# A decode kernel on one core: neighbouring matmuls of the key stage share a weight load, and SyncE waits for the store last

## The chip, the cores and the metric

The kernel runs on one core of a Trainium2 chip. Its time is the device time of the program in microseconds (us); the span of a profile is the time from the first to the last instruction that the profiler saw, about 2 us less (132.1 us in an execution of before that took 133.93 us). PE is the tensor engine (PEld its weight loads), DVE the vector engine, ACT the scalar engine, SyncE or SP the engine that issues the transfers here. Numbers of the form L309 are lines of the kernel.

"Fast" and "slow" are states that an execution is put into by its time.

## The reference, cut to what matters

One token is decoded. Branch A is attention over the last 4,096 cached positions with 32 query heads on 16 key heads; branch B is a dense layer with gelu. A sigmoid gate mixes them.

```python
q = (x @ wq)                                   # 576 x 4096
scores = einsum("bhqd,bhkd->bhqk", q, k) * Dh ** -0.5
o = einsum("bhqk,bhkd->bhqd", softmax(scores), v)
a = o.reshape(...) @ wo                        # 4096 x 576
b = gelu(x @ w1 + b1) @ w2 + b2                # 576 x 4608, 4608 x 576
return g * a + (1 - g) * b
```

With one token, every weight and every cached key and value is read once and used once or twice: 53.6 MB have to come from device memory (the page of before counts 53.62 MB read).

## The kernel before

The transfers are issued in one order by SyncE: w1, wq, eight blocks of keys, the first half of w2, the values, wo, the second half of w2. The key stage takes each block of keys as it lands, transposes it on DVE in two halves, and multiplies it on PE:

```python
for g in range(NG):
    k_t = big.tile([P, 2, SL, Dh], BF16, name="k_t", tag="CDBA"[g])
    for f in range(2):
        ...
        nc.sync.dma_start(out=k_t[:, f, :, :]..., in_=src)
        kt = kt_pool.tile([P, SL * Dh], BF16, name="kt", tag="kt")
        for u in range(2):
            nc.vector.transpose(...)           # L300: two halves of a block
        for u in range(4):
            for j in range(4):                 # L309: 16 matmuls of 512 columns
                nc.tensor.matmul(
                    s_ps[:, u * 512 : (u + 1) * 512]...,
                    lhsT=qz[:, h0 // 2, j, :],
                    rhs=kv[:, u * SL // 4 : (u + 1) * SL // 4, j // 2, :, j % 2],
                    ...
                )
```

Each of these matmuls has its own weight load (`lhsT`), although only four different weights occur in a block. The end of the kernel:

```python
# L415, L417: wo in two pieces, the second half of w2 in pieces of 10, 6 and 2 rows
for r in range(RO):
    y_add(ov[:, r : r + 1], wo_t[:, r, :])               # two matmuls of 288 columns each
for f in range(NJ, NF):
    y_add(gt[:, f : f + 1], w2_t[:, f, :], stop=(f == NF - 1))
out_row = const.tile([1, D], BF16, name="out_row")
nc.scalar.copy(out=out_row[:, DH:D], in_=y_out[1])
nc.vector.tensor_copy(out=out_row[:, 0:DH], in_=y_out[0])
nc.sync.dma_start(out=out..., in_=out_row[:])            # the store
```

After the last line the framework adds the end of the program: SyncE waits for eleven semaphores (counters that the trace shows raised by finished work and waited for), the store's, 103, among them, and then all engines meet in a barrier.

## Time and profile before

| | before |
|---|---|
| time, median (lowest to highest, 5 runs) | 134.09 us (134.00 to 134.19) |
| span of the profile | 132.1 us |
| moved, mean rate | 53.78 MB, 407 GB/s |
| weight loads of the key stage | 128, 12.8 us busy |
| last piece of w2 used from | 128.25 us |
| store issued, span ends | 129.94 us, 132.14 us |

The table of stretches gives for each stretch of time its length, the busy time of each engine (with the number of instructions), the clock granted to PE as a share, the share of time that the transfer engines were busy, and their rate in GB/s.

```profile
44.00:73.00 29.00, 22.71 (x98) 9.16 (x99) 25.09 (x12) 0.00 (x0) 0.00 (x0) 1.00 1.02 432
91.00:113.60 22.60, 14.04 (x498) 13.57 (x495) 0.37 (x3) 0.00 (x0) 0.00 (x0) 0.50 1.00 423
```

The transfers are busy throughout these stretches (shares 1.02 and 1.00), at 432 and 423 GB/s, while PE and DVE have gaps (22.71 and 25.09 us busy of 29.00 in the first, 14.04 and 0.37 of 22.60 in the second), and the chain that ended last is 67% transfers. So the kernel is bound by its reads.

The groups of the key stage, by line, engine, operation and shapes, with count, busy time in us and mean ns of one, and behind the second bar the idle time of the engine before them and what ended it:

```profile
L300 DVE STREAM_TRANSPOSE kt<-k_t 128x2048 f32<-128x2048 f32 x16 | 36.0, 2290 | 9.7 <-DMA k_t<-in_A_k_cache_dram 9.7
L309 PE MATMUL s_ps<-kt,qz_flat 128*128 128x512 bf16 x128 | 32.3, 399 | 9.2 <-DVE kt L300 9.2
L309 PEld LDWEIGHTS <-qz_flat 128*128 128x128 bf16 x128 | 12.8, 100 | 28.3 <-issue 14.7
```

DVE waits for keys to land, PE waits for DVE, and nothing waits for a weight load. The timeline around one half of a block (start, length, engine, line, what, count, and in brackets the idle time before) shows the pace:

```profile
61.33 1.89 PE L309 MATMUL s_ps<-kt,qz_flat 128*128 128x512 bf16 x8 [0.30 <-DVE kt L300]
61.33 1.61 PEld L309 LDWEIGHTS <-qz_flat 128*128 128x128 bf16 x8 [0.58 <-issue]
61.68 4.50 DVE L300 STREAM_TRANSPOSE kt<-k_t 128x2048 f32<-128x2048 f32 x2 [0.41 <-DMA k_t<-in_A_k_cache_dram]
```

Eight matmuls with eight loads take 1.89 us. A matmul's record is 377 ns long, but the records overlap: in this row they start (1.89 - 0.377) / 7 = 0.216 us apart, and 217 ns is the mean of all gaps at full clock in the trace.

The end of the chain that ended last (start, length, what):

```profile
100.84 27.37 DMA w_t<-in_B_w_dram
128.21 0.04 issue
128.25 1.19 PE y_ps L193 x16
129.44 0.44 DVE out_row L437
```

The last pieces of w2 land, 16 output matmuls follow, then the cast and the store. SyncE's wait for the store, from its waits (total, times, longest, in us):

```profile
SPq L464 <- DMA out_dram<-out_row: 0.8, 1, 0.8
```

What stands behind that wait does not show on a page of busy times, because semaphore instructions are not counted as busy. The trace's records of SyncE's own instructions have it (start us, length us, instruction, what it waits for by semaphore; 103 is the store's):

```
 129.940   0.307 DMA_DIRECT2D     the store is issued
 130.304   0.797 EVENT_SEMAPHORE  104, 103
 131.138   0.028 EVENT_SEMAPHORE  105, 102
 131.200   0.028 EVENT_SEMAPHORE  108, 100
 131.264   0.028 EVENT_SEMAPHORE  109, 101
 131.326   0.028 EVENT_SEMAPHORE  110, 107
 131.391   0.007 DRAIN            99
 ...                              barrier of all engines, to 132.139
```

The store has landed at 131.10 us, and five more instructions follow one another, each for semaphores that were satisfied long before.

### The profile page before, as it was taken

How to read it: one execution, taken by the hardware profiler on the slowest of the kernel's cores; microseconds unless marked ns; L12 is line 12 of the kernel's file. 1: busy time of each engine (PE TensorE's matmuls, PEld its weight loads, DVE VectorE, ACT ScalarE, POOL GpSimd, SP SyncE). 2: the span in 40 equal slices, each digit the busy share in tenths (PEclk: the TensorE clock that was granted, in tenths of full speed). 3: DMA queues.
4: the chain of work that ended last, by engine and by line, in shares of the span. 5: the costliest groups of instructions: out<-in, count | busy, mean ns of one | idle time of the engine just before them, and what ended most of it. 6: DMA issues, size and time to landing. Idle time of an engine off the chain costs nothing.

```text
span 132.1 us, 2458 instructions
## 1 busy us (share of the span) xinstructions
PE 77.4 (59%) x1126; PEld 51.1 (39%) x1126; DVE 55.4 (42%) x80; ACT 12.9 (10%) x25; POOL 0.7 (1%) x6
## 2 busy tenths in 40 slices
PE   0038999084699769769779460007942952456651
PEld 0035999084234323223223230007942952333430
DVE  6059100503978988988985710653000000100001
ACT  3000000003000000000000059940000000000001
POOL 2000000000000000000000000000000000000000
PEclk9999999999999999999999996555555555556998
DMA  7999998999999999999999999999999999999960
GB/s 246 421 443 411 448 518 368 398 427 427 427 417 432 422 431 419 427 436 417 454 408 442 451 446 417 407 466 427 397 451 387 431 417 428 429 407 427 406 249 0
DMA packets 3190, 53.78 MB, mean 407 GB/s; under 512 B 358, under 2 KB 362, under 8 KB 620
## 3 DMA queue, kind: packets, MB, share of 16 engines
q1 hardware_dynamic: 3170, 53.61, 95.7%
q8 instruction: 9, 0.15, 0.4%
q10 hardware_dynamic: 10, 0.01, 0.0%
q14 instruction: 1, 0.01, 0.0%
HBM read 53.62 MB, written 0.00 MB: 406 GB/s over the span
## 4 chain that ended last, share of the span: by engine, by line
DMA 67%; PE 12%; DVE 8%; ACT 7%; issue 2%; SPq 1%; DVEq 0%
DMA k_t<-in_A_k_cache_dram 26%; DMA w_t<-in_B_w_dram 21%; DMA wq_t<-in_A_wq_dram 20%; ACT p_t L351 7%; PE o_ps L402 5%; DVE kt L300 3%; PE q_ps L257 3%; DVE pt L359 2%; DVE m L321 2%; PE s_ps L309 1%; PE y_ps L193 1%; SPq L415 1%; PE t_ps L377 0%; DVE out_row L437 0%; SPq L417 0%
## 5 line engine op out<-in xcount | busy, mean ns | idle before, releaser
L300 DVE STREAM_TRANSPOSE kt<-k_t 128x2048 f32<-128x2048 f32 x16 | 36.0, 2290 | 9.7 <-DMA k_t<-in_A_k_cache_dram 9.7
L309 PE MATMUL s_ps<-kt,qz_flat 128*128 128x512 bf16 x128 | 32.3, 399 | 9.2 <-DVE kt L300 9.2
L309 PEld LDWEIGHTS <-qz_flat 128*128 128x128 bf16 x128 | 12.8, 100 | 28.3 <-issue 14.7
L402 PE MATMUL o_ps<-pt,v_t 128*128 128x8 bf16 x512 | 14.6, 168 | 8.5 <-DMA v_t<-in_A_v_cache_dram 6.5
L402 PEld LDWEIGHTS <-v_t 128*128 128x128 bf16 x512 | 14.3, 104 | 8.9 <-DMA v_t<-in_A_v_cache_dram 6.7
L351 ACT ACTIVATE p_t<-s_ps,negm 128x512 bf16<-128x512 f32 x8 | 9.7, 1412 | 44.9 <-DVE negm L342 44.9
L219 PE MATMUL h_ps<-x,w_t 128*128 128x2 bf16 x162 | 10.2, 202 | 0.0
L219 PEld LDWEIGHTS <-w_t 128*128 128x128 bf16 x162 | 10.1, 169 | 0.0
L420 DVE TENSOR_TENSOR om<-o_ps,rgh 128x128 bf16<-128x128 f32 x1 | 0.3, 292 | 22.2 <-PE o_ps L402 22.2
L193 PE MATMUL y_ps<-wo_t,ov 128*1 128x288 bf16 x64 | 6.1, 364 | 4.6 <-DMA wo_t<-in_A_wo_dram 4.6
L359 DVE STREAM_TRANSPOSE pt<-p_t 128x2048 bf16<-128x2048 bf16 x2 | 4.6, 2312 | 7.4 <-ACT p_t L351 7.4
L377 PE MATMUL t_ps<-ls,ones 128*128 128x32 f32 x2 | 0.6, 396 | 11.9 <-DVE ls L375 11.9
L193 PE MATMUL y_ps<-w_t,gt 128*1 128x288 bf16 x72 | 5.6, 285 | 2.1 <-DMA w_t<-in_B_w_dram 2.1
L437 DVE CAST out_row<-y_ps 1x288 bf16<-1x288 f32 x1 | 0.4, 446 | 15.1 <-PE y_ps L193 15.1
L257 PE MATMUL q_ps<-x,wq_t 128*128 128x2 bf16 x144 | 4.0, 166 | 4.0 <-DMA wq_t<-in_A_wq_dram 4.0
L193 PEld LDWEIGHTS <-ov 128*1 128x1 bf16 x64 | 3.4, 103 | 7.0 <-issue 4.5
L257 PEld LDWEIGHTS <-wq_t 128*128 128x128 bf16 x144 | 3.9, 104 | 4.0 <-DMA wq_t<-in_A_wq_dram 4.0
L377 PEld LDWEIGHTS t_ps<-ls,ones 128*128 128x128 f32 x2 | 0.5, 310 | 12.2 <-issue 12.2
L120 PE MATMUL xs_ps<-one_b,rows 1*128 1x1 bf16 x9 | 0.7, 195 | 7.2 <-DVE rows L117 7.2
L193 PEld LDWEIGHTS <-gt 128*1 128x1 bf16 x72 | 3.2, 83 | 3.9 <-issue 2.9
L436 ACT CAST out_row<-y_ps 1x288 bf16<-1x288 f32 x1 | 0.4, 390 | 42.2 <-PE y_ps L193 42.2
L228 DVE COPY hacc<-h_ps 128x36 f32<-128x36 f32 x1 | 0.2, 196 | 9.4 <-PE h_ps L219 9.4
(68 smaller groups left out, 28.7 us busy)
## 6 DMA issues: line engine op xcount, KB each, us to landing
k_t<-in_A_k_cache_dram SPq DMA_DIRECT2D x8, 2048.0 KB, 32.3
v_t<-in_A_v_cache_dram SPq DMA_DIRECT2D x3, 4096.0 KB, 29.8
wq_t<-in_A_wq_dram SPq DMA_DIRECT2D x1, 4608.0 KB, 25.8
wo_t<-in_A_wo_dram SPq DMA_DIRECT2D x2, 2304.0 KB, 20.2
v_t<-in_A_v_cache_dram SPq DMA_DIRECT2D x2, 2048.0 KB
w_t<-in_B_w_dram SPq DMA_DIRECT2D x1, 2880.0 KB, 14.1
w_t<-in_B_w_dram SPq DMA_DIRECT2D x1, 2592.0 KB, 11.3
w_t<-in_B_w_dram SPq DMA_DIRECT2D x1, 2304.0 KB, 8.0
```

Source lines behind the costliest of these rows:

```text
L120: nc.tensor.matmul(xs_ps[:, i : i + 1], lhsT=xdup[:, i : 2 * D : NI], rhs=one_b[0:1, 0:1], start=(i == 0), stop=(i == NI - 1), skip_group_ ...
L193: nc.tensor.matmul(y_out[s], lhsT=vec, rhs=row[:, s * DH : (s + 1) * DH], start=start, stop=stop, skip_group_check=True,)
L219: nc.tensor.matmul(h_ps[:, j:NF:NJ], lhsT=w1_t[:, i, j:FH:NJ], rhs=x2[:, i, :], start=False, stop=(i == NI - 1 and j == NJ - 1), skip_grou ...
L257: nc.tensor.matmul(q_ps[:, j : Hq : Hq // 2], lhsT=wq_t[:, i, j * Dh : (j + 1) * Dh], rhs=x2[:, i, :], start=(i == 0 and j == 0), stop=(i ...
L300: nc.vector.transpose(out=kt[:, u * half : (u + 1) * half].bitcast(FP32), in_=k_t[:, f, u * SL // 2 : (u + 1) * SL // 2, :] .rearrange("p ...
L309: nc.tensor.matmul(s_ps[:, u * 512 : (u + 1) * 512].rearrange("p (c k) -> p c k", k=32), lhsT=qz[:, h0 // 2, j, :], rhs=kv[:, u * SL // 4 ...
L321: nc.vector.reduce_max(out=m2[:], in_=s_ps[:].rearrange("p (n b) -> p b n", b=2), axis=AX.X)
L351: nc.scalar.activation(out=p_t[:, cs, :, b], in_=s_ps[:].rearrange("p (c k u b) -> p u b c k", k=8, u=2, b=2)[:, f, b % 2], func=ACT.Exp, ...
L359: nc.vector.transpose(out=pt[:, cs, :].rearrange("p c h -> p (c h)"), in_=p_t[:, cs, :, :].rearrange("p c k b -> p (c k b)"),)
L377: nc.tensor.matmul(t_ps[:], lhsT=ones[:], rhs=ls[:], start=True, stop=True)
L402: nc.tensor.matmul(o_ps[:, 8 * g : 8 * g + 8, 0], lhsT=v_t[:, c, :], rhs=pt[:, c, 8 * g : 8 * g + 8], start=(c == 0), stop=(c == NCK - 1),)
L415: nc.sync.dma_start(out=wo_t[:, r0:r1, :], in_=wo_src[:, r0:r1, :])
```

## The change

The intent: leave out weight loads that repeat the one before, and let the waits that are satisfied anyway run while the store is still in flight. The loop of the key stage is turned so that two matmuls with the same weights follow each other; a pass over the finished program drops a load whose weights are already in place; a second pass sorts the eleven waits so that the store's is left for the last instruction, the drain.

```diff
+    def keep_weights(nc):
+        body = nc.main_func.blocks[1]
+        loaded, kept = None, []
+        for i in body.instructions:
+            if type(i).__name__ == "InstLdweights":
+                ...                                  # key: address, pattern, tile position
+                free = sync is None or not (sync.on_wait or sync.on_update)
+                if key == loaded and free:
+                    continue
+                loaded = key
+            elif type(i).__name__ == "InstMatmult" and i.ldweights is not False:
+                loaded = None
+            kept.append(i)
+        body.instructions = kept
+
+    def store_wait_last(nc):
+        ...
+        waits = list(drain.sync_info.on_wait)
+        waits.sort(key=lambda w: w.id != sem)        # the first of the list stays on the drain
+        ...
-            for u in range(4):
+            for half in range(2):
                 for j in range(4):
-                    nc.tensor.matmul(
-                        s_ps[:, u * 512 : (u + 1) * 512]...
+                    for u in (2 * half, 2 * half + 1):
+                        nc.tensor.matmul(
+                            s_ps[:, u * 512 : (u + 1) * 512]...
```

## The prediction

Two passages are cut from the prediction, where it is marked. That no load is waited for rests on the waits of the trace (all of PE's 9.2 us of idle time in that group ended with DVE).

> **What bounds the kernel.** Transfers. The page shows 406 GB/s over the 132.1 us span; the table of stretches gives a DMA share of 0.99 to 1.02 and 423 to 432 GB/s from 34 to 113.6 us.[...] The chain that ended last is 67% DMA, 12% PE. SyncE issues the last load at 101.3 us and it lands by 128.2 us; nothing in the middle counts unless it starves that queue. After the last w2 piece lands come 16 output matmuls (1.15 us), the cast (0.45 us), the store's issue (0.31 us) and the end of the program, at 132.1 us.

> **Part 1, key stage.** The loop order makes two neighbouring matmuls share their weights, so the second load of each pair goes: 64 of 128, none of which carries a semaphore in the trace. The 128 loads were 12.8 us busy (100 ns each), so 6.4 us of weight-load busy time goes. None of it is waited for: matmuls at full clock start 216 to 217 ns apart with a load between each[...]. The first ones, at half clock, are 425 to 428 ns apart. So 8 matmuls stay at 1.89 us. PE also waits there: per 4.9 us of arriving keys it needs 3.8 us, and DVE's two transposes (2.29 us each) take 4.5 of it. Worth 0.00 to 0.05 us inside the stage and nothing on the span.

> **Part 2, end.** The trace's records of SyncE's own instructions show the order now: one semaphore instruction waits for the store (with another semaphore) from 130.30 to 131.10 us; then four more at 62 to 65 ns each, at 131.14, 131.20, 131.26 and 131.33; the drain at 131.39. With the store's semaphore moved to the drain, five pair waits run while the store is in flight (5 x 62 = 0.31 us, inside its 0.80 us), and the drain starts at about 131.10 to 131.14. All on the critical path: 0.25 to 0.29 us saved.

> **Sum.** 134.09 - 0.27 = 133.8 us, range 133.5 to 134.1: 0.2%.

> **What would show it.** Part 1: 64 loads in the group of qz weights, busy about 6.2 us; matmuls of s_ps x128 still 376 to 378 ns and 216 ns apart; the reduction of s_ps starting at the same time, within 0.2 us. Part 2: the drain starts within 0.05 us of the store's landing; store's issue to the span's end takes 1.9 us, not 2.2. The last w2 landing is unchanged.

> **What would make it wrong.** (a) The clock: at 34.2 us the key stage starts at half clock and gets full clock from about 39.2 us; it falls to half at 80 and rises at 121. Should fewer loads delay full clock, 16 matmuls of two key blocks need 6.8 us against 4.9 us of arrival, and late buffers could starve the queue: I give that 1%. (b) A shifted phase of the clock's steps may run the last 16 output matmuls at half clock, about +0.9 us. (c) The transfer rate differs by more than 0.27 us; before's runs spread 0.1 us. (d) If the drain takes the wait more slowly than a semaphore instruction, part 2 shrinks.

## The result

The median is 133.73 us (133.56 to 133.76, 5 runs) against 134.09 us (134.00 to 134.19, 5 runs). Ratios are computed as the mean time of one kernel's fast runs over that of the other's of the same rounds, so not quite the ratio of the medians quoted: 0.997 here, with a 95% interval of 0.9957 to 0.9984. It is faster, by 0.3%. The prediction was 133.8 us with a range of 133.5 to 134.1.

The lines of the profile after, in the same order. The stretches:

```profile
44.00:73.00 29.00, 22.80 (x98) 4.62 (x51) 25.02 (x13) 0.00 (x0) 0.00 (x0) 1.00 1.02 433
91.00:113.60 22.60, 13.66 (x491) 13.33 (x489) 0.28 (x1) 0.00 (x0) 0.00 (x0) 0.50 1.00 423
```

The weight loads' busy time in the key stage is halved (9.16 to 4.62 us), and the rate of the transfers is what it was. The groups:

```profile
L341 DVE STREAM_TRANSPOSE kt<-k_t 128x2048 f32<-128x2048 f32 x16 | 36.0, 2291 | 9.8 <-DMA k_t<-in_A_k_cache_dram 9.8
L351 PE MATMUL s_ps<-kt,qz_flat 128*128 128x512 bf16 x128 | 32.0, 397 | 9.2 <-DVE kt L341 9.2
L351 PEld LDWEIGHTS <-qz_flat 128*128 128x128 bf16 x64 | 6.4, 100 | 34.2 <-issue 33.0
```

64 loads and 6.4 us are gone from PEld; PE waits for DVE 9.2 us as before, and DVE for the keys 9.8 us. One half of a block in the timeline:

```profile
61.24 1.89 PE L351 MATMUL s_ps<-kt,qz_flat 128*128 128x512 bf16 x8 [0.29 <-DVE kt L341]
```

Eight matmuls still take 1.89 us. After this change some matmuls have a load before them and some have none, so one trace holds the cost of a hidden load: at full clock 46 gaps with a load have a mean of 217.4 ns, and 58 gaps without one 216.7 ns. A load costs 0.7 ns here, 0.05 us for all 64. The end of the chain, and SyncE's wait:

```profile
103.91 24.41 DMA w_t<-in_B_w_dram
128.32 0.04 issue
128.36 1.19 PE y_ps L234 x16
129.55 0.44 DVE out_row L479
```

```profile
SPq L506 <- DMA out_dram<-out_row: 0.5, 1, 0.5
```

The last pieces of w2 are used from 128.36 us, 0.1 us later than in the trace of before: the middle has given nothing in this pair of traces. The gain is behind it. SyncE's own instructions after:

```
 130.048   0.314 DMA_DIRECT2D     the store is issued
 130.419   0.027 EVENT_SEMAPHORE  104, 102
 ...                              four more, at 130.48, 130.54, 130.61 and 130.67
 131.196   0.007 DRAIN            103
 ...                              barrier of all engines, to 131.944
```

From the store's issue to the end of the span it was 132.139 - 129.940 = 2.20 us, and is now 131.944 - 130.048 = 1.90 us: 0.30 us.

### The profile page after: what moved, and what is told of

It is laid out like the page before. It is cut to its first block, busy times and chain, and to the rows that moved or that the text cites. A ratio compares the mean times of both kernels' runs of the same rounds, so it can differ in the third digit from the quotient of the medians.

```text
span 131.9 us, 2394 instructions
## 1 busy us (share of the span) xinstructions
PE 76.9 (58%) x1126; PEld 44.6 (34%) x1062; DVE 55.4 (42%) x80; ACT 12.9 (10%) x25; POOL 0.7 (1%) x6
## 4 chain that ended last, share of the span: by engine, by line
DMA 64%; PE 12%; DVE 8%; ACT 7%; issue 5%; SPq 1%; DVEq 0%
DMA k_t<-in_A_k_cache_dram 26%; DMA wq_t<-in_A_wq_dram 20%; DMA w_t<-in_B_w_dram 18%; ACT p_t L393 7%; PE o_ps L444 5%; DVE kt L341 3%; PE q_ps L298 3%; DVE pt L401 2%; DVE m L363 2%; PE s_ps L351 1%; PE y_ps L234 1%; SPq L457 1%; PE t_ps L419 0%; SPq L459 0%; DVE out_row L479 0%
## 5 line engine op out<-in xcount | busy, mean ns | idle before, releaser
L351 PEld LDWEIGHTS <-qz_flat 128*128 128x128 bf16 x64 | 6.4, 100 | 34.2 <-issue 33.0
```

Of the source, the lines that this page charges most:

```text
L351: nc.tensor.matmul(s_ps[:, u * 512 : (u + 1) * 512].rearrange("p (c k) -> p c k", k=32), lhsT=qz[:, h0 // 2, j, :], rhs=kv[:, u * SL // 4 ...
```

## The experiments

Three questions were open. Is the end the whole of the gain, when the medians of this first comparison differ by 0.36 us and the end gives 0.30? Is a weight load really free? And what does the rest of the spread come from? Theory A says: all of the gain is the end; the loads are hidden. Rivals are named where they were put to a test. "Issue to end" is the time from the store's issue to the end of the span in the run's own trace.

| run | what | median us (lowest to highest) | before, same rounds | ratio (95%) | issue to end, us |
|---|---|---|---|---|---|
| e1 | key stage's part alone | 134.05 (133.91 to 134.86) | 134.09 | 0.9999 (0.9969 to 1.0029) | 2.20 |
| e2 | the end's part alone | 133.88 (133.73 to 134.66) | 134.09 | 0.9994 (0.9964 to 1.0023) | 1.89 |
| e3 | the whole change again | 133.79 (133.57 to 135.56) | 134.09 | 0.9995 (0.9951 to 1.0038) | 1.90 |
| e4 | loop order alone, 128 loads | 134.19 (134.01 to 135.09) | 134.09 | 1.0017 (0.9987 to 1.0047) | 2.20 |
| e5 | two loads per matmul | 135.28 (135.10 to 135.38) | 134.05 | 1.0089 (1.0074 to 1.0104) | 2.20 |
| e6 | four loads per matmul | 135.37 (135.32 to 136.36) | 134.05 | 1.0096 (1.0079 to 1.0113) | 2.20 |
| e7 | 6 pairs of waits more, mostly ahead of the store's | 134.40 (133.93 to 134.98) | 134.05 | 1.0027 (0.9992 to 1.0062) | 2.18 |
| e8 | 6 pairs more, store's wait last | 133.75 (133.66 to 134.10) | 134.05 | 0.9982 (0.9967 to 0.9996) | 1.90 |
| e12 | 6 pairs more, all behind the store's | 134.31 (134.23 to 134.57) | 134.06 | 1.0011 (0.9970 to 1.0052) | 2.57 |
| e9 | the change and 192 idle PE instructions | 135.32 (135.11 to 135.58) | 134.06 | 1.0095 (1.0082 to 1.0108) | 1.90 |
| e10 | the change, wo's rows cut unevenly | 142.97 (141.03 to 143.47), two slow | 134.06 | 1.0619 (1.0573 to 1.0664) | 1.89 |
| e11 | the change, PE kept busy near the end | 133.79 (133.57 to 133.98) | 134.06 | 0.9978 (0.9967 to 0.9990) | 1.90 |

All twelve kernels gave correct results.

### e1 to e4: each part alone

e1 takes the change without `store_wait_last`; e2 takes the kernel before with nothing but that pass; e4 takes the new loop alone.

```diff
-    nc.at_finalize(keep_weights)      # e2, e4
-    nc.at_finalize(store_wait_last)   # e1, e4
```

> Weight loads left out and the loop reordered, end of the program as before. Theory A (the whole gain is the end of the program): 134.05 to 134.10 us, within 0.05 us of before; from the store's issue to the end of the span 2.20 us, as before. Rival B (part of the gain comes from 64 fewer PE instructions, by way of one 16 KB program fetch fewer, the one at 128.2 us in the trace of before): 133.95 to 134.00 us, about 0.1 us under before. Rival C (the loads themselves were waited for): 133.8 or less.

> The key stage as before with its 128 loads, only the order of SyncE's last waits changed. Theory A: 0.28 to 0.36 us under before, the same as the whole change; from the store's issue to the end of the span 1.90 us. Rival B: 0.25 to 0.30 us under before, clearly less than the whole change. Rival C: no more than 0.1 us under before.

> The whole change once more, beside its parts on the same chip. All theories: 0.3 to 0.4 us under before. Theory A: equal to the second kernel within 0.05 us. Rival B: 0.1 us under the second kernel.

> The key stage's loop in the new order, all 128 loads kept, end as before. Theory A and rival B: before within 0.05 us, matmuls at full clock 217 ns apart. If this alone is faster by 0.1 us, the order counts and not the loads.

In the traces the end parts the kernels cleanly: 2.20 us from issue to end in both that keep the old order, 1.89 and 1.90 us in both that change it. The medians follow: 0.04 us for the key stage alone, 0.21 us for the end alone, 0.30 us for both, and 0.1 us the other way for the loop alone. The means do not follow, and none of the four ratios is clear of 1: each kernel, the one before too, had one or two executions in six to eleven that were 0.6 to 1.8 us longer, and they fell unevenly. What the ones that a profile caught were comes below (e11). Rival C, that the loads themselves were waited for, falls. Rival B, that the key stage's part gives 0.1 us, is not refuted by these numbers: 0.04 us between medians whose runs scatter by 0.1 us can't tell 0 from 0.1. Two other records speak against it: e8 below has the old key stage with its 128 loads and is 0.30 us under its kernel before, as much as the whole change; and the last landing is no earlier without the 64 loads (end of e9).

### e7, e8, e12: waits ahead of the store's and behind it

```diff
+        again = [next(w for w in waits if w.id != sem)] * 6
+        waits = waits[:1] + again + waits[1:] + again      # e12; e7 and e8 put 12 at the end of the list
```

> The kernel before with six more pairs of semaphore waits, all long satisfied, behind the wait for the store. Theory A (62 ns each, on the path): from the store's issue to the end of the span 2.20 + 0.37 = 2.57 us, time 134.45 us. Rival (satisfied waits are free and the end is bound by the store): 2.20 us.

> The same six pairs more, but with the store's wait last, on the drain. Eleven pairs are 0.69 us, inside the 0.78 us between the end of the store's issue and its landing. Theory A: 1.90 us from the store's issue to the end of the span, time as with the changed order alone, 133.8 us. Rival (each instruction costs its time wherever it stands): 2.27 us.

> The run with late waits missed its aim: its trace shows that seven of its eleven pairs came before or with the store's wait and only four after it, as in the kernel before, and it took 2.18 us from the store's issue to the end of the span. Now the store's pair is the first and ten satisfied pairs stand behind it, six more than before. Theory A (62 ns for each pair behind the store): 2.20 + 0.37 = 2.57 us from the store's issue to the end of the span, time 134.4 us. Rival (satisfied waits are free): 2.20 us, 134.05 us.

SyncE's own instructions in e8, and in e12:

```
 130.066   0.318 DMA_DIRECT2D     e8: the store is issued
 130.435   0.028 EVENT_SEMAPHORE  the first of eleven pairs, the last at 131.049
 131.219   0.007 DRAIN            103

 129.941   0.322 DMA_DIRECT2D     e12: the store is issued
 130.314   0.788 EVENT_SEMAPHORE  104, 103
 131.139   0.028 EVENT_SEMAPHORE  the first of ten pairs, the last at 131.689
 131.754   0.013 DRAIN            99
```

e7 was not the kernel that its expectation speaks of. The framework seems to pair the waits from both halves of the list (before has 104 with 103 and 105 with 102, the kernel after 104 with 102 and 105 with 100), and the trace showed six pairs ahead of the store's wait and four behind it, as before. It took 2.18 us, so six pairs more ahead of the store cost nothing. e8 has eleven pairs ahead and none behind: 1.90 us, the same as with five. e12 is what e7 was meant to be, ten pairs behind: the expectation was 2.57 us and the trace has 132.508 - 129.941 = 2.57 us. The same twelve waits more cost 0.37 us in one place and nothing in the other, where all eleven pairs fit between the store's issue and the drain 1.15 us after it. It is the position that costs, 62 ns for each pair behind the landing (0.37 us for six).

### e5, e6: more weight loads

```diff
+            if type(i).__name__ == "InstLdweights" and "qz_flat" in str(i.ins[0].memref):
+                out.append(i)
+                for n in range(EXTRA):                 # 1 in e5, 3 in e6
+                    out.append(copy.replace(i, name=..., sync_info=None))
```

> The kernel before with every weight load of the key stage issued twice (256 loads). Theory A (loads of 96 ns are hidden under matmuls that start 217 ns apart): two loads need 192 ns and still hide, matmuls at full clock 215 to 220 ns apart, stage and time as before within 0.1 us. Rival[...]: 310 ns apart, 8 matmuls in 2.55 us in place of 1.90, which with two blocks per 4.9 us still just overtakes the transfers; time up by the last block's 0.65 us at most on the softmax chain, not on the span.

The rival's 310 ns are about the 217 ns of the gap and the 96 ns of a second load together, an estimate.

> Every weight load of the key stage issued four times (512 loads). Theory A: 4 x 96 = 384 ns of loads per matmul no longer hide: matmuls about 385 ns apart, 8 of them 2.9 to 3.1 us, 16 in 6.0 us against 4.9 us between key blocks, so the stage ends 5 to 10 us later than 73 us; the span grows only if the later release of the key buffers starves the queue of transfers: within 2% of before, 0 to 2 us. Rival: matmuls stay 217 ns apart (a repeated load costs nothing): time as before.

The matmuls at full clock start 219 ns apart with two loads each, and 223 ns apart with four. The group of e6:

```profile
L328 PE MATMUL s_ps<-kt,qz_flat 128*128 128x512 bf16 x128 | 32.1, 395 | 9.2 <-DVE kt L319 9.1
L328 PEld LDWEIGHTS <-qz_flat 128*128 128x128 bf16 x512 | 28.1, 97 | 12.9 <-issue 9.9 <-ACT qz_flat L298 1.3
```

My expectation of 385 ns for four loads was wrong, and it was wrong by reading the 97 ns of a load's record as the time for which it holds the engine. In the trace the four records of a group start 40 ns apart and overlap: four take 4 x 40 = 160 ns (an estimate from these starts), less than the 217 ns between the starts of two matmuls in before. The rival of e5, 310 ns with two loads, falls as well. So a load of these weights was hidden here even fourfold, up to 6 ns a matmul (223 against 217 ns), and leaving one of two out had nothing to give in this stage. The reduction behind the key stage starts at 73.0 to 73.3 us in all of before, after, e5 and e6.

And yet both kernels are slower, by 1.2 to 1.3 us in the median and by 1.0 us or more in every execution, and hardly more with four loads than with two. Neither theory had said why: the expectation of e6 had room for 0 to 2 us, but by key buffers that come free late.

### e9: where 1.2 us came from

The chain of e5 ends with w2 landing late:

```profile
101.28 28.10 DMA w_t<-in_B_w_dram
129.38 0.04 issue
129.42 1.19 PE y_ps L212 x16
```

129.38 us in place of 128.21 in the kernel before. More reads of data there were not. But PE's program was longer, and the table of queues lists transfers of instructions, in packets of 16 KB (16,384 bytes in the records of before). That they fetch PE's program is read from their number: eight in the kernel after, nine with 64 PE instructions more (before) or 192 more (e9), ten with 448 more (e6). The lines give packets, MB and the share of 16 engines. Before:

```profile
q8 instruction: 9, 0.15, 0.4%
```

After:

```profile
q8 instruction: 8, 0.13, 0.4%
```

e6:

```profile
q8 instruction: 10, 0.16, 0.5%
```

e9 puts it to the test without touching the key stage, with loads of one column in a stretch where PE has nothing to do:

```diff
+        again = [copy.replace(load, name=f"I-{3000000 + n}", sync_info=None) for n in range(192)]
+        body.instructions = body.instructions[:at] + again + body.instructions[at:]
```

> The whole change, plus 192 weight loads of one column put into PE's idle gap between 78 and 90 us, where nothing waits for them; the key stage keeps its 64 loads. Theory F (each 16 KB fetch of PE program takes 1.55 us of one transfer engine; the first eight fall on eight engines, a ninth before the last landing falls on one of them again): nine fetches before 128 us, the last at about 121 us as with doubled loads, one of the 16 engines ending about 1.2 us after the others, time 1.2 to 1.3 us over the change, 134.9 to 135.1 us. Rival (in the kernels with doubled and fourfold loads it was the loads' own reads that slowed the transfers): no more than 0.1 us over the change, 133.8 us.

```profile
77.34 3.02 PEld L250 LDWEIGHTS <-gt 128*1 128x1 bf16 x202
90.02 0.08 PEld L250 LDWEIGHTS <-gt 128*1 128x1 bf16 x1 [9.66 <-DVE ls L433]
117.25 4.00 PE L250 MATMUL y_ps<-wo_t,ov 128*1 128x288 bf16 x32 [3.04 <-DMA wo_t<-in_A_wo_dram]
123.89 4.00 PE L250 MATMUL y_ps<-wo_t,ov 128*1 128x288 bf16 x32 [2.64 <-DMA wo_t<-in_A_wo_dram]
127.68 3.34 PE L250 MATMUL y_ps<-w_t,gt 128*1 128x288 bf16 x36
```

The 192 loads are done by 80.4 us and PE then waits 9.7 us more, so they delay nothing themselves (the first of these lines). Nine fetches come before 128 us, the ninth at 121.16. Its effect is in the fourth line: the second half of wo is used from 123.89 us, where the kernel after had 122.77. The last completion is at 129.73 us, and only one engine is so late: all others are done by 128.57 us, 1.2 us earlier, as expected. The time is 135.32 us, about 1.5 us over the change; I had expected 1.2 to 1.3. In this trace PE is still at half clock when the late piece comes (full clock from 129.64 us, in the kernel after from 120.74), so that it, and not the landing, is the last to finish: the last two lines follow on without a wait. The landing is 1.13 us later than in the kernel after; the other 0.4 us is left for the half clock, which no run separates from the fetch. The rival, that the loads' own reads had slowed the transfers, falls.

So leaving out instructions does have a worth in this kernel, but in steps: 192 PE instructions more than the change has cost 1.5 us (135.32 against 133.79 us), while the 64 fewer than before only moved a fetch that started at 128.21 us out of the program, where it delayed little or nothing: with that ninth fetch (before, e2, e4, e7, e8, e12) the last completion comes at 128.38 to 128.56 us, without it (after, e1, e11) at 128.60 to 128.67, and later in e3.

### e10: an attempt to use the idle engines, failed

Theory F says that eight engines are done 1.4 us before the others. e10 tried to give them more of wo, by loading its second half in pieces of 112, 8 and 8 rows. The author meant eight engines to carry one row of 18 KB less by this, and eight one more. Which engines take which rows no trace shows, so the times of 133.1 and 134.4 us are estimates that rest on it.

```diff
-    for r0, r1 in ((0, 16), (16, RO)):
+    for p0, p1, r0, r1 in ((0, P, 0, 16), (0, 112, 16, RO), (112, 120, 16, RO), (120, P, 16, RO)):
```

> The whole change, with the second half of wo loaded as 112 rows[...] and twice 8 rows[...]. Theory F says eight engines end 1.4 us late. If those are the eight that now carry less, all 16 end within 0.4 us of each other, the last landing at about 127.8 us in place of 128.4, time 133.1 us. If they are the eight that carry more, the last landing at 129.1 us, time 134.4 us; if mixed, the same as that. Rival (the two groups are an artefact and the engines share one rate): no change, 133.75 us.

It was 6% slower, outside all of the expectations. The stretches of its trace:

```profile
112.00:118.00 6.00, 1.99 (x63) 1.81 (x61) 0.48 (x2) 0.00 (x0) 0.00 (x0) 0.50 1.04 338
118.00:124.00 6.00, 4.00 (x32) 1.93 (x31) 0.00 (x0) 0.00 (x0) 0.00 (x0) 0.50 1.02 230
124.00:130.00 6.00, 0.00 (x0) 0.00 (x0) 0.00 (x0) 0.00 (x0) 0.00 (x0) 0.50 0.95 161
```

The engines are as busy as ever (shares 1.04, 1.02 and 0.95), at 338, 230 and 161 GB/s, where the first two of these stretches had 433 and 411 in before: packets of 18 KB, 0.69 us long before, last mostly 1.2 to 1.4 us while the 112 rows are under way. It is not these rows alone: the packets of the two pieces of 8 rows took 1.5 us and more, and those of w2 behind them, a transfer of 128 rows, about 1.0 us in place of 0.435 until the small pieces had landed. Which of the three pieces slows the transfers, and how, was not settled, and whether the two groups of engines can be evened out stays open.

### e11: the executions that are 0.9 us longer

The profile of e2 happened to fall on such an execution. PE's last lines there:

```profile
126.19 1.39 PE L215 MATMUL y_ps<-w_t,gt 128*1 128x288 bf16 x20 [1.36 <-DMA w_t<-in_B_w_dram]
128.31 2.08 PE L215 MATMUL y_ps<-w_t,gt 128*1 128x288 bf16 x16 [0.73 <-DMA w_t<-in_B_w_dram]
```

and its stretch behind 128 us, where the clock is the third number from the right:

```profile
128.00:130.00 2.00, 1.69 (x16) 0.87 (x15) 0.00 (x0) 0.00 (x0) 0.00 (x0) 0.52 0.10 34
```

The same 16 matmuls that took 1.15 us at full clock take 2.08 us: the clock fell to half at 128.09 us, while PE was waiting for the last piece. In the trace of before it fell at 131.3 us, when all was done. The profiles of e6 and e7 show the same 2.08 us. This was risk (b) of the prediction. e11 keeps PE busy in the gaps, with ten matmuls whose results nobody reads:

```diff
+    def keep_warm(row, n):
+        for _ in range(n):
+            nc.tensor.matmul(s_ps[:, 0:512], lhsT=ident[:], rhs=row[:, 0:512], start=True, stop=True)
     for r in range(RO):
         y_add(ov[:, r : r + 1], wo_t[:, r, :])
+        if r % 16 == 15:
+            keep_warm(wo_t[:, r, :], 4)
     ...
+        if f == NJ + 9:
+            keep_warm(w2_t[:, f, :], 2)
```

> The whole change, plus ten matmuls of 512 columns into dead PSUM, four behind each half of wo and two behind the first piece of w2, while PE waits for transfers. Theory H (some executions run their last 16 output matmuls at half clock, 2.08 us in place of 1.15): with PE busy in the gaps no execution does, all within 133.5 to 134.0 us, median 133.75 us. Rival (those slow executions come from the transfers): the share of executions 0.8 us over the median stays as before, about one in five.

All five executions lie within 133.57 to 133.98 us, with the same median as the change without it. That agrees with theory H, but it does not prove the cure: in these rounds none of the eleven executions of the kernel before was a long one either. What is shown is the cause of a long execution where a profile caught it (e2, e6, e7). The profile of e3, at 134.34 us, is a long execution of another kind: one engine's last completion came at 129.21 us, 0.5 us behind all others, with full clock at the end and with eight fetches. Its cause is open. One packet of w2's first half, at 64.26 us, took 1.07 us longer than others of its size; but e11 has such a packet too (1.08 us) and was not long. No version came out that is clearly faster than the change.

## Why the prediction was right, point by point

- **What bounds the kernel.** Right: the rate of the transfers (432 and 433 GB/s in the key stage) and PE's waits (9.2 us) are the same before and after, and the last pieces of w2 are used from 128.25 and 128.36 us.
- **Part 1 worth nothing.** Right for the loads: 64 gone, 6.4 us of PEld busy time (6.2 predicted as what remains, and 6.4 measured for that too), matmuls 217 ns apart, the reduction behind them at 73.07 and 72.99 us. The trace has 216.7 ns without a load and 217.4 ns with one, so the expectation holds by this comparison within one trace. e5 and e6 show that there was room for four loads (219 and 223 ns). A worth of up to 0.1 us by another way could not be excluded, since the change's median was 0.09 us better than the end's part alone (133.79 against 133.88 us), which is no more than the scatter; but e8, with the end's part and 128 loads, was at 133.75 us.
- **Part 2, 0.25 to 0.29 us.** Right in kind, and slightly small: 0.30 us in the traces (2.20 to 1.90 us from issue to end, as predicted). The drain started at the store's landing itself, with no step between (landing recorded at 131.179 us, drain at 131.196). e12 confirms the 62 ns of each pair.
- **The sum.** 133.8 us predicted, 133.73 and 133.79 us measured.
- **"Nothing in the middle counts unless it starves that queue."** Incomplete, though it cost nothing here. e9 and e5 show that the middle also counts through the fetches of PE's program, which by the reconstruction take turns with the data on the transfer engines, 1.55 us each: had the 64 loads been what made a ninth fetch fall before 128 us, taking them out would, by these two (1.2 and 1.5 us), have been worth over 1 us, an estimate.
- **Risk (b), half clock at the end.** It did not touch the first comparison, which was luck (of the six executions of e2, two were long ones, and the profile of one of them shows this cause), and showed in later profiles with the size given, 0.93 us (2.08 - 1.15).

## What to carry to other kernels

At the end of a program, order the waits so that the one that is satisfied last comes last: here each satisfied pair behind it cost 62 ns on the critical path (e12), and in front of it nothing, where they fitted into the flight (e8: eleven pairs, 0.69 us, before a drain 1.15 us after the issue). Busy time of weight loads was no estimate of what leaving them out gives (6.4 us gone, 0.7 ns between matmuls gained); look at the gap between the starts of two matmuls, and at what PE waits for. In a kernel that is bound by its transfers, count the program's own fetches too: here 64 PE instructions fewer gave nothing that the traces show, and in the kernels in which a ninth fetch fell before 128 us (e5, e6, e9) the medians were 1.2 to 1.5 us longer.
